# Larger transfers and merged DMA transposes in a one-core kernel for a speech joint network, forward and backward

The chip is one Trainium2, and the kernel uses one of its cores. The metric is device time in microseconds (us) of one execution on that core. Nearly all executions of one kernel fall within a few us; the few that are more than 1.5% above the fastest of their kernel are called slow and are left out of every comparison.

## The reference

The forward part is two convolutions over time with stride 2 and GELU, two projections, and a "joint" of every time step with every one of the 8 label positions `u`. The kernel returns this output and the gradients of all seven inputs, for a given `grad_out`.

```python
# x [2, 16000, 256], w1 and w2 [3, 256, 256], g [2, 8, 256], w_f, w_g, w_o [256, 256]; bf16
h  = gelu(conv(x, w1))[:, ::2]                  # 8000 steps
f  = gelu(conv(h, w2))[:, ::2]                  # 4000 steps
j  = tanh((f @ w_f)[:, :, None] + (g @ w_g)[:, None])
out = j @ w_o                                   # [2, 4000, 8, 256]
_, vjp = jax.vjp(forward, x, w1, w2, g, w_f, w_g, w_o)
return out, *vjp(grad_out)                      # grad_out [2, 4000, 8, 256]
```

## The kernel before

The 8000 rows of the joint are cut into 18 chunks (14 of 512 rows, two of 256, two of 160). A chunk has four pairs of `u`. For each pair, `grad_out` is loaded as rows (`GO_R`), which the gradient of `w_o` uses directly, and transposed by DMA into columns (`GOT`), which TensorE needs for the gradient of `j`. Rows of h, f and their gradients, needed for the weight gradients, are made by DMA transposes too. All these transposes are issued by one engine, SyncE (SP), one after the other.

The kernel orders its own instructions. Each operation is handed to a scheduler (`Flow`) with a cost in ns, and the scheduler simulates the engines and emits an order for each. The cost of a transpose is flat: 1260 ns, whatever its size.

```python
def dma(q, out, in_, r, w, bytes_, ..., transpose=False, ...):
    ...
    c = 1260.0 if transpose else 400.0 if q == "SP" else cost or (750.0 if q == "POOL" else 100.0)
    return op(q, c, go, r=r, w=w, ..., work=bytes_ / 256 * 1.25 if transpose else bytes_ / 300.0)
# ... cut: buffer classes, with their number of slots (some of 37)
("jt", 3), ("got", 3), ("go", 7), ("out", 6), ("rows", 4), ("hro", 2), ("hrs", 2), ("hre", 2), ("fr", 2),
# ... cut
def load_got(g_, up, h, at):            # half h (256 rows) of one pair of u: 8 blocks of 128x128
    if h == 0:
        S.setdefault("GOT", {})[up] = buf("got", [P, NB, 2, KT, P], BF16, "GOT")
    GOT, GO = S["GOT"][up], S["GO"][up, h]
    dma("SP", lambda: GOT[:, 2 * h:2 * h + 2].rearrange("p a u k q -> p (a u k) q"),
        lambda: GO[:].rearrange("p a u v -> p (a u v)"), r=[GO], w=[(GOT, h)], bytes_=2 * P * 1024,
        new=[GOT] if h == 0 else [], transpose=True, ...)

def load_gor(g_, up, h, at, hold=()):
    GO = buf("go", [P, 2, 2, V], BF16, "GO_R")
    # ... cut: one load of 256 KB per half
# ... cut: gradient of h, odd columns, in two products because the shifted block is a tile of its own
for q_, (lo, hi, in0) in enumerate(((0, P, lambda mt=mt: S["G1S"][:, mt, :]),
                                    (P, Ws, lambda mt=mt: S["G1o"][:, mt, r0:r0 + Ws - P]))):
    op("DVE", c_dve(hi - lo), ... scalar_tensor_tensor(out=GHo[:, mt, lo:hi], ...))
# ... cut: one transpose each for the rows of h (three) and of grad h (two)
GHoR = dma_rows("GHoR", "rows", g_, lambda: GHo[:]..., ghok, nb_of[g_])
GHeR = col_rows("GHeR", "rows", g_, GHe, ["z"])
```

## Time and profile before

| | before |
|---|---|
| median of 3 runs | 803.32 us (801.99 to 803.36) |
| span of the profiled execution | 800.2 us |
| TensorE busy, VectorE, ScalarE, GpSimd | 775.6, 754.2, 715.2, 223.2 us |
| SP queue taken by DMA issues, added up over the trace | 700.4 us, 494 issues |

This is SP's timeline before, around 120 us (columns: start, time that the issue took on the queue, operation, destination and source, count). "SPq" marks the queue itself.

```profile
113.86 3.74 SPq L438 DMA_TRANSPOSE GOT<-GO_R  x2
117.70 1.26 SPq L438 DMA_TRANSPOSE GHoR<-GHo  x1
119.02 1.34 SPq L438 DMA_TRANSPOSE GOT<-GO_R  x1
120.45 1.28 SPq L438 DMA_TRANSPOSE GHeR<-GHe  x1
121.83 3.79 SPq L438 DMA_TRANSPOSE GOT<-GO_R  x2
```

The halves of `GOT` stand between the other transposes, and the queue comes back to one of them every 5.2 us in the median over the run. The view of the tile `GOT` gives the issue times over the whole run (ns: least, median, most):

```profile
L438 SPq DMA_TRANSPOSE GOT<-GO_R x128: 1231/1436/4699, 19.4 to 765.8; - x128
```

### The profile page before, as it was taken

The numbers are of one execution on the slowest core, as the hardware profiler recorded it, in microseconds if no ns is written. First come the engines' busy times: TensorE is split into PE (matmuls) and PEld (weight loads), VectorE is DVE, ScalarE is ACT, GpSimd is POOL, SyncE is SP. The second block draws the span as 40 slices with busy tenths as digits, with TensorE's granted clock in tenths as the row PEclk, the third lists the DMA queues.
The fourth block names the chain that finished last, engine by engine and source line by source line (L and its number), as shares of the span: only waits on it lengthen the run. The fifth ranks groups of instructions, "written<-read, shape, count | busy, mean of one in ns | idle before, by whom it ended". The sixth has DMA issues, their size and how long they took to land.

```text
span 800.2 us, 17623 instructions
## 1 busy us (share of the span) xinstructions
PE 775.6 (97%) x6196; PEld 576.2 (72%) x6196; DVE 754.2 (94%) x1756; ACT 715.2 (89%) x1164; POOL 223.2 (28%) x461
## 2 busy tenths in 40 slices
PE   8788999999999999999999999999999999999997
PEld 6555667686776867787776668676776767778885
DVE  5999999998989999997989999999999999999995
ACT  5999999999898999997899999989898999898572
POOL 1212222321323122343232142222223122233242
PEclk9999999999999999999999999999999999999999
DMA  8999999999999998999999999999999999999984
GB/s 202 242 206 207 216 263 253 229 249 275 228 243 261 224 254 185 230 253 250 224 200 236 252 236 242 251 209 255 245 236 248 217 247 229 245 215 263 195 205 114
DMA packets 384700, 184.74 MB, mean 231 GB/s; under 512 B 331716, under 2 KB 368358, under 8 KB 384612
## 3 DMA queue, kind: packets, MB, share of 16 engines
q1 hardware_dynamic: 366644, 133.25, 85.8%
q0 software_dynamic: 15584, 49.19, 19.7%
q10 hardware_dynamic: 2384, 1.18, 0.6%
q8 instruction: 48, 0.79, 0.4%
q14 instruction: 40, 0.33, 0.1%
HBM read 52.48 MB, written 50.34 MB: 128 GB/s over the span
## 4 chain that ended last, share of the span: by engine, by line
PE 68%; DVE 19%; ACT 10%; issue 2%; DMA 1%; DVEq 0%; ACTq 0%
PE ps L412 58%; PE GWO L412 9%; DVE NGZ L833 4%; DVE ZS L841 3%; ACT JT L766 2%; DVE g_s L599 2%; DVE JR L779 2%; ACT JR L786 2%; DVE ACC L894 1%; ACT g_sq L595 1%; ACT JSQ L823 1%; DVE g_sq L610 1%; ACT g_s L605 1%; DVE GHo L954 1%; DMA XC<-in_x_dram 1%
## 5 line engine op out<-in xcount | busy, mean ns | idle before, releaser
L766 ACT ACTIVATE JT<-FE,GE 128x512 bf16<-128x512 bf16 (+2 forms) x288 | 182.0, 676 | 5.8 <-PE ps L412 5.6
L440 POOL DMA_DIRECT2D out_dram<-OUT_SB x136 | 95.2, 701 | 241.8 <-ACT OUT_SB L423 153.8
L412 PE MATMUL ps<-WO,JT 128*128 128x256 bf16 x1024 | 151.4, 272 | 2.7 <-DVE NGZ L833 0.8
L833 DVE SCALAR_TENSOR_TENSOR NGZ<-JSQ,ps 128x512 f32<-128x512 bf16 (+2 forms) x252 | 151.0, 605 | 2.0 <-PE ps L412 1.8
L412 PE MATMUL ps<-GOT,WT 128*128 128x512 bf16 (+3 forms) x640 | 151.0, 332 | 1.2 <-ACT HTe L597 0.5
L786 ACT ACTIVATE JR<-JR 128x1024 bf16<-128x1024 bf16 x128 | 136.4, 1070 | 6.6 <-DVE JR L779 6.5
L412 PE MATMUL GWO<-GO_R,JR 128*128 128x256 bf16 x1024 | 132.2, 273 | 3.3 <-ACT JR L786 3.3
L823 ACT ACTIVATE JSQ<-JT 128x1024 bf16<-128x1024 bf16 (+2 forms) x132 | 126.6, 960 | 7.7 <-DVE NGZ L833 5.7
L412 PEld LDWEIGHTS <-JT 128*128 128x128 bf16 x1024 | 98.4, 98 | 47.7 <-issue 5.7
L841 DVE TENSOR_TENSOR ZS<-ZS,NGZ 128x512 f32<-128x512 f32 (+2 forms) x216 | 131.1, 614 | 0.1
L423 ACT CAST OUT_SB<-ps 128x512 bf16<-128x512 f32 x208 | 119.2, 598 | 8.4 <-PE ps L412 8.2
L412 PEld LDWEIGHTS <-JR 128*128 128x128 bf16 x1028 | 99.5, 98 | 26.4 <-ACT JR L786 4.7
L412 PEld LDWEIGHTS <-WT 128*128 128x128 bf16 x1000 | 88.1, 98 | 37.3 <-issue 2.3
L412 PEld LDWEIGHTS <-W 128*128 128x128 bf16 x792 | 70.4, 99 | 56.8 <-issue 3.7
L412 PE MATMUL ps<-XC,W 128*128 128x512 bf16 (+4 forms) x432 | 94.2, 347 | 3.0 <-DMA XC<-in_x_dram 2.1
L779 DVE TENSOR_TENSOR JR<-FER,GEB 128x1024 bf16<-128x1024 bf16 x128 | 87.5, 685 | 0.1
L440 POOL DMA_DIRECT2D out_dram<-GX_SB x70 | 39.0, 558 | 159.6 <-ACT GX_SB L425 125.0
L412 PEld LDWEIGHTS <-X 128*128 128x128 bf16 x768 | 74.9, 98 | 10.8 <-DMA HRs<-HTo 0.2
L599 DVE SCALAR_TENSOR_TENSOR g_s<-g_sq,ps 128x512 bf16<-128x512 bf16 (+2 forms) x108 | 65.7, 609 | 11.7 <-ACT HTo L597 9.2
L412 PE MATMUL ps<-WT,GHo 128*128 128x256 bf16 x384 | 73.0, 273 | 0.2
L894 DVE TENSOR_TENSOR ACC<-ACC,ps 128x512 f32<-128x512 f32 x96 | 64.2, 677 | 9.2 <-PE ps L412 9.0
L595 ACT ACTIVATE g_sq<-ps 128x512 bf16<-128x512 f32 (+2 forms) x108 | 58.5, 546 | 10.1 <-PE ps L412 9.7
(137 smaller groups left out, 1281.5 us busy)
## 6 DMA issues: line engine op xcount, KB each, us to landing
GO_R<-in_grad_out_dram SPq DMA_DIRECT2D x120, 256.0 KB, 4.2
out_dram<-OUT_SB POOLq DMA_DIRECT2D x120, 256.0 KB, 4.8
X<-in_x_dram SPq DMA_DIRECT2D x28, 576.0 KB, 7.0
out_dram<-GX_SB POOLq DMA_DIRECT2D x60, 256.0 KB, 4.6
GOT<-GO_R SPq DMA_TRANSPOSE x128, 5.2
out_dram<-w_out SPq DMA_DIRECT2D x9, 128.0 KB, 2.1
GO_R<-in_grad_out_dram SPq DMA_DIRECT2D x8, 128.0 KB, 4.3
out_dram<-OUT_SB POOLq DMA_DIRECT2D x8, 128.0 KB, 3.8
```

Of the source, the lines that this page charges most:

```text
L412: nc.tensor.matmul(ps_ap, lhsT=lhsT, rhs=rhs, start=start, stop=stop)
L423: nc.scalar.copy(out=dst(), in_=src())
L440: return eng_.dma_start(out=out(), in_=in_())
L595: op("ACT", c_act(W, True), lambda e, mt=mt, ps=ps: nc.scalar.activation(out=sq[:, mt, :W], in_=ps[:, :W], func=ACT.Square, scale=GELU_SQR ...
L599: op("DVE", c_dve(W), lambda e, mt=mt, ps=ps: nc.vector.scalar_tensor_tensor(out=s[:, mt, :W], in0=sq[:, mt, :W], scalar=1.0, in1=ps[:, :W ...
L766: op("ACT", c_act(W, ptr=True), lambda e, j=j, mt=mt: nc.scalar.activation(out=JT[:, j, mt, :W], in_=S["FE"][:, mt, :W], func=ACT.Tanh, bi ...
L779: op("DVE", c_dve(n * 2 * D, 0.5), lambda e, lo=lo, n=n, m=m, JR=JR: nc.vector.tensor_tensor(out=JR[:m, lo % 2:lo % 2 + n], in0=S["FER"][: ...
L786: op("ACT", c_act(n * 2 * D), lambda e, lo=lo, n=n, m=m, JR=JR: nc.scalar.activation(out=JR[:m, lo % 2:lo % 2 + n], in_=JR[:m, lo % 2:lo % ...
L823: nc.scalar.activation(out=JSQ[:, :, :W], in_=JT[:, j, :, :W], func=ACT.Square)
L833: op("DVE", c_dve(W) + 6, lambda e, d2=d2, ps=ps, u=u, zap=zap, JSQ=JSQ: nc.vector.scalar_tensor_tensor(out=zap(), in0=JSQ[:, d2, :W], sca ...
L841: op("DVE", c_dve(W), lambda e, d2=d2, dst=dst, NGZ=NGZ: nc.vector.tensor_tensor(out=dst[:, d2, :W], in0=ZS[:, d2, :W], in1=NGZ[:, :W], op ...
L894: op("DVE", c_dve(512), lambda e: nc.vector.tensor_tensor(out=acc_ap().rearrange("p k d -> p (k d)"), in0=acc_ap().rearrange("p k d -> p ( ...
```

## The change

The intent is fewer and larger transfers. `grad_out`, its transpose and the output go by whole pairs of `u`, 512 rows at a time. Grad x is stored for two row blocks at once. The rows of h come out of one transpose of 18 blocks, and those of grad h out of one of 16. The block of h that is shifted by one column is kept in h's own tile, so convolution 2 reads it in one matmul and grad h is one product. Slots are recounted to fit the memory. The core of the diff:

```diff
-                    ("hto", 2), ("hs", 2), ... ("got", 3), ("go", 7), ("out", 6), ("rows", 4), ("hro", 2), ("hrs", 2), ("hre", 2), ("fr", 2) ...
+                    ("hh", 2), ... ("got", 3), ("go", 4), ("out", 3), ("rows", 2), ("ghr", 1), ("hr", 1), ("hrs", 1), ("fr", 1) ...
-    def load_got(g_, up, h, at):
-        dma("SP", lambda: GOT[:, 2 * h:2 * h + 2]..., lambda: GO[:]..., bytes_=2 * P * 1024, ...)
+    def load_got(g_, up, at):
+        S, n = st[g_], nb_of[g_]
+        GOT, GO = buf("got", [P, NB, 2, KT, P], BF16, "GOT"), S["GO"][up]
+        dma("SP", lambda: GOT[:, 0:n]..., lambda: GO[:, 0:n]..., bytes_=n * P * 1024, new=[GOT], transpose=True, ...)
-        GO = buf("go", [P, 2, 2, V], BF16, "GO_R")
+        GO = st[g_].setdefault("GO", {})[up] = buf("go", [P, NB, 2, V], BF16, "GO_R")
... (cut: out and grad x likewise)
+        HT = buf("hh", [P, KT * (2 * CW + P)], BF16, "HT")          # odd, shifted and even h in one tile
-        HRo = col_rows("HRo", "hro", g_, HTo, ["z"], late[0])
-        R0 = dma_rows("HRs", "hrs", g_, lambda: HS[:]..., [HS], 1, late[0])
-        HRe = col_rows("HRe", "hre", g_, HTe, ["z"], late[1])
+        dma("SP", lambda: HR.t[:, 0:ns + nc_]..., lambda: HT.t[:, 0:ns + nc_], r=[HT], w=[HR], ..., transpose=True, nb=late[0])
-        GHoR = dma_rows("GHoR", ...); GHeR = col_rows("GHeR", ...)
+        dma("SP", lambda: GHR.t[:, 0:2 * nc_]..., lambda: GH.t[:, 0:2 * nc_], r=ghk, w=[GHR], ..., transpose=True)
-            for q_, (lo, hi, in0) in enumerate(((0, P, ...G1S...), (P, Ws, ...G1o...))):
-                op("DVE", c_dve(hi - lo), ...)
+            op("DVE", c_dve(Ws), ...)
```

## The prediction

> **What bounds the kernel now.** I read the page first (busy shares, slices, chain of waits), then the busy time by stretches of 20 us, then the waits of TensorE and of the SP queue, then single tiles.
>
> The page's busy shares, its two slice rows for TensorE and DMA, and its chain:
>
> ```profile
> span 800.2 us, 17623 instructions
> PE 775.6 (97%) x6196; PEld 576.2 (72%) x6196; DVE 754.2 (94%) x1756; ACT 715.2 (89%) x1164; POOL 223.2 (28%) x461
> ...
> PE   8788999999999999999999999999999999999997
> ...
> DMA  8999999999999998999999999999999999999984
> ...
> PE 68%; DVE 19%; ACT 10%; issue 2%; DMA 1%; DVEq 0%; ACTq 0%
> ```
>
> TensorE is busy 775.6 of 800.2 us. DMA is as full as TensorE in these rows, but holds 1% of the chain: transfers arrive in time. The by-stretch view (columns: stretch and length, then TensorE, weight loads, VectorE, ScalarE, GpSimd, granted clock, DMA share, GB/s) shows where TensorE's missing 24.6 us are:
>
> ```profile
> 0.00:20.00 20.00, 16.37 (x141) 12.47 (x142) 10.02 (x33) 11.11 (x24) 3.52 (x16) 0.91 0.83 202
> 20.00:40.00 20.00, 15.86 (x123) 10.88 (x121) 19.49 (x55) 20.00 (x39) 5.16 (x10) 1.00 1.16 242
> 40.00:60.00 20.00, 17.23 (x130) 11.71 (x129) 19.64 (x55) 19.61 (x33) 3.24 (x8) 1.00 0.96 206
> 60.00:80.00 20.00, 17.46 (x131) 11.94 (x130) 20.00 (x46) 19.70 (x30) 4.67 (x10) 1.00 1.04 207
> ...
> 780.00:800.00 20.00, 14.77 (x139) 11.41 (x136) 11.50 (x31) 4.71 (x10) 5.74 (x14) 0.98 0.44 115
> ```
>
> The first four stretches lack 3.6 + 4.1 + 2.8 + 2.5 = 13.0 us, the last 5.2; the 700 us between lack 6.4. From 20 to 80 us VectorE and ScalarE are full, and TensorE waits for them. TensorE's waits name only two on a DMA:
>
> ```profile
> PE GWO L412 <- ACT JR L786: 3.3, 3, 1.5
> PE psb L652 <- DVE FE L428: 3.2, 4, 1.6
> ...
> PE ps L412 <- DMA XC<-in_x_dram: 2.1, 1, 2.1
> ...
> PE ps L412 <- DMA GOT<-GO_R: 0.4, 1, 0.4
> ```
>
> The 2.1 us are the very first load of x, which the change leaves alone. So what this change makes cheaper, transfers, costs TensorE 0.4 us that can be seen.
>
> [...] six 512-column matmuls starting at 499.64 are followed by the next group at 500.93, so 1.29 / 6 = 215 ns[...]. [...] start and end (about 7 us before the first x is in, some 5 at the end) can't be streamed over.
> [...] grad_out loads land after 4.2 us at 256 KB and still 3.8 us at 32 KB.
> [...]
> [...] the grad-h product takes 277 ns at 128 columns, 543 at 384 and 677 at 512, so a line of 1.04 ns per column over about 144 ns.
>
> **The change, part by part** (18 chunks: 14 of 512 rows, two of 256, two of 160).
> - *Fewer grad_out loads and transposes.* 136 loads become 80 (14 x 4 + 2 x 4 + 2 x 4 x 2) and 128 transposes 72. A load issue takes 0.53 us and a transpose at least 1.23 us of the SP queue even for few blocks (the 16-block one of x 1.46), so SP gets back about 56 x 0.53 + 56 x 1.2 = 97 us. The merged h transposes take 58 issues to 22, grad h 36 to 18: 54 x 1.2 = 65 us. SP spends much of its time waiting for others (79.0 us for the matmuls ahead of transposes alone), and TensorE loses 0.4 us to it. Worth: about 0.
> - *Fewer stores.* Out stores go from 136 (701 ns of GpSimd) to 80, large grad x stores from 60 (558 ns) to about 30. From 256 against 128 row pieces I get 143 ns per 128 pieces, so a doubled out store is about 1.0 us; GpSimd saves roughly 95 - 56 x 1.0 - 24 x 0.6 = 25 us plus 15 us. It is busy 28% and mostly waits for ScalarE's output. Worth: about 0.
> - *The shifted block in h's own tile.* Convolution 2 streams one 512-column matmul where it had 128 + 384: 72 fewer matmuls, same columns[...].
> - *grad h (odd) in one product.* Per full chunk and half 277 + 543 becomes 677 ns: 143 ns; 36 of them are 5.2 us of VectorE's 754. VectorE holds 19% of the chain; 0.19 x 5.2 = 1.0 us, and in the last chunk, where this product stands alone on the chain, 272 + 178 becomes about 310: 0.1 us. Worth: about 1.1 us.
> - *The end.* The two last grad-h transposes are issued at 787.64 and 788.93 and the last gradients wait for both; one issue saves up to 1.2 us, of which its longer flight takes some back. Worth: 0.5 us.
> - *Buffers.* 7 half slots of grad_out become 4 whole ones, 6 of out become 3, so a chunk of 256 or 160 rows, which fills only half a slot or less, now has 4 in place of 7. Before, SP issues seven grad_out loads at 13 to 18 us: four for chunk 0 and three for chunk 1. Now chunk 0 takes all four, and chunk 1's first must wait for the first gradient-of-w_o matmuls (25 to 26 us). Behind that SP is in two x transposes until 33.7, then come a load (about 5 us) and a transpose (about 6): ready at about 45 us, first used at 50.6 now. It just fits, or costs 1 to 4 us in the stretch where VectorE and ScalarE are already the limit. I book 1.5 us.
> Sum: -0.2 - 1.1 - 0.5 + 1.5 = about -0.3 us on the span. The instruction order is also made anew by the kernel's own scheduler, whose model of transfers changes; that moves things by a few us either way, without a sign I can give. The reported 803.32 is itself one of 801.99 to 803.36, with the profiled run at 801.93. Prediction: 801.0 us, a trifle better as the buffer cost may not show.
>
> **Rivals.**
> - *DMA relief is worth more than it looks.* For: DMA is at nine tenths in nearly all slices, and transposes at times hold SP for 2.8 us (median of those of x), a sign of a full path. Against: bytes are the same, the packets under 512 B (331716 of 384700) come from the transposes and are not made larger, and TensorE waits 0.4 us. Were all of TensorE's 6.4 us gaps in the middle due to it, the time would be 795.
> - *Buffers become the bound.* Coarser slots (out, grad_out, one slot each for the h, grad-h and f rows) make TensorE wait at each chunk. For: fewer slots, held for a whole pair. Against: a pair lasts 12 us (48 us per chunk over 4), an out slot is held 12 + 5 us, and three slots give 36; the h rows are loaded about a chunk ahead and read in the first third of the next. If it bit in all 18 chunks by 1 us: 819.
> - *VectorE was the true limit.* Then the whole 5.2 us come off: 796. Against: in the middle TensorE shows 20.00 of 20 in most stretches.
>
> **Range and chances.** Faster by over 2% means under 787: two thirds of all of TensorE's idle time gone, from a change that touches 0.4 us of its waits: 0.03. Slower by over 2% means 16 us of new waits, only by the buffer rival in most chunks: 0.07. The rest, 0.90. The range of 791 to 811 leaves 10 us each way for the new order and the start.
>
> **What would show each step right or wrong.** Right: TensorE busy at 774 to 777 us; 72 fewer matmuls; VectorE down by 5 us to about 749; GpSimd down by 30 to 45; SP issues nearly halved with no wait of TensorE on them. The start is right if the stretches 20 to 60 lack 6 to 11 us. Wrong if the waits show TensorE on grad_out's transposes or on DMA for more than 3 us (buffers), or if the stretches between 120 and 780 lack clearly more or less than 5 us. A gap that repeats once per chunk would refute me most.

## The result, and the profile after

The changed kernel takes 812.14 us (median of 4 runs, 808.41 to 814.33), against 803.34 us (801.99 to 804.06) for the kernel before, run on the same chip. The ratio is 1.0107, with a 95% interval of 1.0067 to 1.0147. All ratios here are the mean time of one kernel's fast runs over that of the other's of the same rounds, so they are not quite the ratios of the medians quoted. It counts as "same" at 2%, but it is 1% slower and lies 1.1 us above the predicted range. The profiled execution, at 814.33 us, is the slowest of the four, and that of the kernel before, at 801.93 us, among its fastest: the spans compared below differ by 12.4 us, the medians by 8.8.

The page after:

```profile
span 812.6 us, 16872 instructions
PE 780.9 (96%) x6124; PEld 575.1 (71%) x6124; DVE 744.4 (92%) x1710; ACT 716.5 (88%) x1179; POOL 154.2 (19%) x370
...
PE 42%; DVE 25%; ACT 22%; DMA 5%; issue 5%; SPq 1%; DVEq 0%; ACTq 0%
```

There are 72 fewer matmuls, as planned, and 10 and 69 us less work on VectorE and GpSimd. Yet TensorE is busy for 5.3 us longer, and its share of the chain fell from 68 to 42%. The stretches of 20 us (stretch and length, then TensorE, weight loads, VectorE, ScalarE, GpSimd, granted clock, DMA share, GB/s) show one place, first after and then before:

```profile
120.00:140.00 20.00, 15.76 (x133) 12.73 (x131) 16.62 (x37) 18.25 (x27) 2.88 (x6) 1.00 1.17 182
140.00:160.00 20.00, 18.96 (x105) 10.67 (x106) 14.83 (x30) 14.05 (x23) 2.27 (x5) 0.83 1.06 262
```

```profile
120.00:140.00 20.00, 20.00 (x166) 15.81 (x165) 19.20 (x40) 19.30 (x31) 5.11 (x8) 1.00 1.12 253
140.00:160.00 20.00, 20.00 (x136) 12.70 (x135) 19.29 (x44) 19.07 (x30) 6.06 (x13) 1.00 1.05 229
```

Before, TensorE worked through all 40 us at full clock. After, it lacks 4.24 and 1.04 us, and in the second stretch the mean clock is 0.83. TensorE's waits and its timeline name what it lacked (in brackets: idle time just before, and what ended it):

```profile
PE ps L412 <- DMA GOT<-GO_R: 5.3, 1, 5.3
```

```profile
141.04 1.03 PE L412 MATMUL ps<-GOT,WT 128*128 128x512 bf16 x2 [5.28 <-DMA GOT<-GO_R]
```

It is a single wait of 5.28 us for a transposed pair of `grad_out`. The records of the granted clock show 6.8 us at half speed from 140.0 on, 4.2 us into the wait. In the 5.8 us of it that lie after the wait, matmuls of 512 columns start 427 ns apart, against 216 ns in the microseconds after; these 5.8 us cost another 2.9 us, as an estimate (half of them). SP's timeline shows why the pair was late:

```profile
116.06 3.59 SPq L438 DMA_TRANSPOSE GHR<-GH  x1
119.75 1.25 SPq L438 DMA_TRANSPOSE FR<-FT  x1
121.05 0.58 SPq L440 DMA_DIRECT2D GO_R<-in_grad_out_dram  x1
121.73 4.53 SPq L438 DMA_TRANSPOSE HR<-HT  x1
126.36 9.43 SPq L438 DMA_TRANSPOSE GOT<-GO_R  x1
```

Everything that the issue at 126.36 had to wait for had happened by 119.70 (read from the semaphores in the trace). So it stood behind the merged transposes of grad h and h, and then took 9.43 us itself. What made it take so long can be read in part from GpSimd's timeline, which shows three stores of 512 KB in the 7 us around:

```profile
122.11 0.59 POOL L440 DMA_DIRECT2D out_dram<-GX_SB  x1 [6.40 <-ACT GX_SB L425]
123.07 0.71 POOL L440 DMA_DIRECT2D out_dram<-OUT_SB  x1 [0.37 <-ACT OUT_SB L423]
128.13 0.55 POOL L440 DMA_DIRECT2D out_dram<-GX_SB  x1 [4.36 <-DVE ZS L863]
```

The packets of the DMA engines, which the trace also keeps (128 packets of 256 bytes are one block of a transpose), show these stores moving from 125 to 140 us without a break. From 126 to 138 us the transposes advanced by 1.5 blocks per us, against 3.0 over the whole run. Such slow spells are general here. Between 60 and 760 us, in the microseconds in which any transpose ran, 4.5 blocks per us moved before and 5.2 after where no store did, and 1.9 before but 1.3 after where stores held over half of the engines' time. So the change's larger stores are part of the setting of the stall.

The tile's issue times after:

```profile
L438 SPq DMA_TRANSPOSE GOT<-GO_R x72: 1237/3758/9427, 17.4 to 781.2; - x72
```

Twice the size (16 of the 72 still have 8 blocks) has 2.6 times the median. Added up over the trace, SP's issues took 688.2 us for 328 transfers, against 700.4 us for 494 before. So 166 fewer issues gave back 12 us: the 56 fewer loads of `grad_out` 39 us, while the transposes, 110 fewer, took 24 us more (586.4 to 610.4), and the loads of x 3 us more. Per block of 128x128 the transposes took 0.24 to 0.25 us of the queue in both kernels, each with about 2460 blocks.

Where did the 12.4 us of span go? TensorE's idle time rose by 7.1 us: -0.9 in the first 80 us, +6.4 from 80 to 780 us (5.3 of it the one wait), +1.7 at the end. Its busy time rose by 5.3 us. The clock was at half for 13.8 us of the span, against 4.5 us before, and half of that difference, 4.6 us, is the most that it can have added.

### The profile page after: what moved, and what is told of

The parts are those of the page before. It is cut to its first block, busy times and chain, and to the rows that moved or that the text cites.

```text
span 812.6 us, 16872 instructions
## 1 busy us (share of the span) xinstructions
PE 780.9 (96%) x6124; PEld 575.1 (71%) x6124; DVE 744.4 (92%) x1710; ACT 716.5 (88%) x1179; POOL 154.2 (19%) x370
## 4 chain that ended last, share of the span: by engine, by line
PE 42%; DVE 25%; ACT 22%; DMA 5%; issue 5%; SPq 1%; DVEq 0%; ACTq 0%
PE ps L412 35%; PE GWO L412 6%; DVE NGZ L855 4%; ACT JT L788 4%; ACT JR L808 4%; DVE g_s L603 4%; DVE ZS L863 3%; ACT OUT_SB L423 3%; ACT JSQ L845 2%; ACT g_sq L599 2%; DMA GOT<-GO_R 2%; ACT GX_SB L425 2%; DVE g_sq L614 2%; DVE JR L801 1%; ACT g_s L609 1%
## 5 line engine op out<-in xcount | busy, mean ns | idle before, releaser
L788 ACT ACTIVATE JT<-FE,GE 128x512 bf16<-128x512 bf16 (+2 forms) x288 | 189.9, 705 | 1.5 <-DVE FE L428 1.5
L808 ACT ACTIVATE JR<-JR 128x1024 bf16<-128x1024 bf16 x128 | 139.5, 1100 | 9.8 <-DVE JR L801 9.6
L845 ACT ACTIVATE JSQ<-JT 128x1024 bf16<-128x1024 bf16 (+2 forms) x120 | 118.9, 991 | 16.2 <-DVE NGZ L855 15.4
L423 ACT CAST OUT_SB<-ps 128x512 bf16<-128x512 f32 x204 | 123.8, 614 | 8.6 <-PE ps L412 8.5
L412 PEld LDWEIGHTS <-W 128*128 128x128 bf16 x720 | 66.2, 98 | 55.0 <-issue 3.3
L440 POOL DMA_DIRECT2D out_dram<-OUT_SB x80 | 54.3, 679 | 259.6 <-ACT OUT_SB L423 173.7
L412 PE MATMUL ps<-WT,GH 128*128 128x256 bf16 x732 | 97.9, 275 | 0.2
L412 PE MATMUL ps<-GHR,X 128*128 128x256 bf16 x768 | 92.0, 273 | 0.4 <-DVE NGZ L855 0.4
L412 PEld LDWEIGHTS <-GH 128*128 128x128 bf16 x732 | 72.0, 99 | 12.4 <-DVE GH L971 0.4
L603 DVE SCALAR_TENSOR_TENSOR g_s<-g_sq,ps 128x512 bf16<-128x512 bf16 (+2 forms) x108 | 66.2, 613 | 15.3 <-ACT HT L601 12.7
L599 ACT ACTIVATE g_sq<-ps 128x512 bf16<-128x512 f32 (+2 forms) x108 | 62.2, 576 | 15.8 <-PE ps L412 15.3
```

What stands on the lines that cost most here:

```text
L412: nc.tensor.matmul(ps_ap, lhsT=lhsT, rhs=rhs, start=start, stop=stop)
L423: nc.scalar.copy(out=dst(), in_=src())
L440: return eng_.dma_start(out=out(), in_=in_())
L599: op("ACT", c_act(W, True), lambda e, mt=mt, ps=ps: nc.scalar.activation(out=sq[:, mt, :W], in_=ps[:, :W], func=ACT.Square, scale=GELU_SQR ...
L603: op("DVE", c_dve(W), lambda e, mt=mt, ps=ps: nc.vector.scalar_tensor_tensor(out=s[:, mt, :W], in0=sq[:, mt, :W], scalar=1.0, in1=ps[:, :W ...
L788: op("ACT", c_act(W, ptr=True), lambda e, j=j, mt=mt: nc.scalar.activation(out=JT[:, j, mt, :W], in_=S["FE"][:, mt, :W], func=ACT.Tanh, bi ...
```

## The experiments

Three theories stood after the result.
- **M**, the order: the scheduler charges a flat 1260 ns per transpose, so it doesn't see that a merged one takes twice as long, and queues too much ahead of an urgent one.
- **S**, the size: a 16-block transpose holds the queue and lands late as one piece.
- **B**, the buffers: four whole slots of `grad_out` for seven halves leave too little room.

A fourth, **T**, came later: any order is a draw from a lottery, and the kernel before had been tuned to a good one.

### First three runs

`a_cost158`: the changed kernel, charged by block, so that the order is made anew.

```diff
-        c = 1260.0 if transpose else ...
+        c = max(1260.0, bytes_ / 32768 * 157.5) if transpose else ...
```

> The changed kernel with one number of its own scheduler altered: a transpose is charged to the SP queue by its blocks (157.5 ns each, so 1260 ns for 8 blocks and 2520 for 16) and no longer a flat 1260 ns whatever its size. Transfers, buffers and arithmetic are as in the changed kernel; only the order of instructions can differ. Theory M (the flat charge made the scheduler believe that the merged transposes cost the SP queue half, so that it lines them up too late): the 5.3 us wait of TensorE for GOT at 141 us and the half clock after it are gone, time 800 to 805. Theory S (the 16-block transfer itself is the trouble: its first half can't be used before its second has landed) and theory B (coarser buffers): a wait of 3 us or more for GOT stays, 808 to 814.

Measured: 806.15 us (804.58 to 810.12), ratio 1.0064 [1.0030, 1.0099]. The long wait is gone in its profile, which M wanted, but the time is above M's range and below that of S and B.

`a_halves`: the changed kernel in exactly its own order on every engine; each 16-block transpose of `grad_out` is issued as two of 8, back to back.

```diff
+                eng_.dma_start_transpose(out=o_[:, 0:n // 2], in_=i_[:, 0:n // 2 * P])
+                return eng_.dma_start_transpose(out=o_[:, n // 2:n], in_=i_[:, n // 2 * P:n * P])
```

> The changed kernel in its own order, but each 16-block transpose of grad_out is issued as two of 8 blocks, one right after the other, into the two halves of the same tile. Theory S: the first half lands some 4 us earlier, but the matmuls read the whole tile, so at best the second half lands a little earlier by pipelining: the wait for GOT falls to 3 us or less, time 805 to 809. Theory M: the queue is behind by its order and its bytes, and these are the same: the wait stays within 4 to 7 us, time 808 to 815. Issue time: if the cost went per issue, two of 8 blocks would occupy SP for more than one of 16 (2 x 1.85 against 3.9 us by the two profiles: no difference).

Measured: 807.66 us (806.02 to 810.08), ratio 1.0078 [1.0046, 1.0110]. The longest wait on `GOT` was 1.83 us. That pleased S, but a later run took most of it back.

`b_cheap`: the kernel before, with the charge made too low for its own 8-block transposes.

```diff
+        c = 1260.0 * min(1.0, bytes_ / 524288) if transpose else ...
```

> The kernel before, with its scheduler's charge for a transpose made too small in the same proportion: 78.75 ns per block, so 630 ns for 8 blocks and, as before, 1260 for 16. Transfers and buffers are those of the kernel before. Theory M: the order turns as optimistic as that of the changed kernel, a wait of TensorE on a transpose of 2 us or more appears, 806 to 815. Theories S and B: nothing changes but the luck of the order, 800 to 806 and less than 1 us of waits on GOT.

Measured: 807.17 us (805.15 to 807.59), ratio 1.0064 [1.0035, 1.0094], with a wait of 3.15 us on `GOT` at 28 us. An order made with too low a charge can slow the kernel before as well.

### A control, both cures, and a neutral step

`c_after`: the changed kernel unchanged, as a control.

> The changed kernel itself again, on whatever chip this call gets, as the control for the other runs of this call. Both theories: 808 to 814 us, ratio 1.008 to 1.014 to the kernel before, and TensorE's wait of 4 to 7 us on the transposed grad_out near 141 us is there again, because the order of the instructions on each queue is fixed when the kernel is built. If the wait is gone, it was an accident of one execution and the explanation by queue order falls.

Measured: 810.98 us (806.31 to 816.27), ratio 1.0101 [1.0059, 1.0144]. The loss is there again, but not at the same place. I had expected the wait near 141 us; it was near 744 us:

```profile
744.51 0.61 PE L412 MATMUL ps<-GOT,WT 128*128 128x256 bf16 x2 [9.91 <-DMA GOT<-GO_R]
```

```profile
711.01 9.28 SPq L438 DMA_TRANSPOSE GHR<-GH  x1
720.34 0.58 SPq L440 DMA_DIRECT2D GO_R<-in_grad_out_dram  x1
721.03 1.27 SPq L438 DMA_TRANSPOSE FR<-FT  x1
722.39 8.67 SPq L438 DMA_TRANSPOSE HR<-HT  x1
731.15 4.66 SPq L438 DMA_TRANSPOSE GOT<-GO_R  x1
```

This is the same sequence, a chunk's merged transposes and then an urgent `GOT`, with the length now in the merged ones. The clock was at half for 10.2 us from 737.0 on, 2.4 us into the wait of 9.91 us. The order of the program is fixed and such a sequence comes in every full chunk, so two executions can stall in different chunks, where the transposes happen to take long. The six fast executions fall into two groups, 806.3 to 807.7 and 814.3 to 816.3 us. The 8 us between them is about what the first stall cost with its half clock (5.3 + 2.9). The profiled execution is from the upper group.

`c_halves158` (both cures of the first runs) and `c_pieces158` (the same order, with the transposes of h and grad h in pieces of at most 8 blocks as well):

> The changed kernel with both cures together: its own scheduler charges the transpose queue 157.5 ns per 128x128 block instead of a flat 1260 ns per transfer, and every 16-block transpose of grad_out is issued as two of 8 blocks back to back. Theory M+S (the loss is the flat charge and the long 16-block transposes): 802 to 805 us, ratio 1.000 to 1.005, no wait of more than 1.5 us on transposed grad_out. Rival B (the buffers, counted by whole pairs, and the reordering that comes with them cost the rest): 806 to 809 us, no better than either cure alone (806.15 and 807.66), ratio 1.006 to 1.009.

Measured: 805.80 us (803.62 to 807.98), ratio 1.0035 [1.0014, 1.0056].

> As the run before it, and the merged transposes of h (18 blocks) and of grad h (16 blocks) are issued in pieces of at most 8 blocks too; buffers and order as in that run. If long transposes are what hurts: 801 to 804 us, 1 to 2 us better than with grad_out's alone. If only the transposes that TensorE waits for soon matter (grad_out's), the same within 1 us. If pieces cost the queue something each (34 more issues at 1.2 us or so, hidden so far), still no more than 1 us.

Measured: 803.69 us (803.08 to 810.22), ratio 1.0023 [0.9994, 1.0053]. Neither profile has a wait of 1.5 us on `GOT`. Together the cures win most of the loss back.

`b_1500`: the kernel before, with a flat 1500 in place of 1260.

> The kernel before with only the scheduler's flat charge moved from 1260 to 1500 ns per transpose: no buffer, transfer or instruction changes, only the order in which the scheduler places them. It measures what a reordering without any reason costs. Theory T (the kernel before sits on a tuned order, and any other order costs some 0.5%): 804 to 807 us, ratio 1.004 to 1.008. Theory M (only a charge that is too low hurts, and 1500 is nearer to the measured mean of 1.85 us): 799 to 803 us, ratio 0.997 to 1.002.

Measured: 801.31 us (800.32 to 802.80), ratio 0.9979 [0.9957, 1.0000]. This new order doesn't cost the kernel before anything, which speaks against T. (Over all runs, two of its four new orders are level, this one and `b_late240`, and two cost 0.6 and 0.7%, `b_cheap` and `b_cost240`. So an order can cost half of the loss by itself.)

### Pieces alone, and a fuller charge

`e_pieces`: the changed kernel in exactly its own order, all merged transposes in pieces of at most 8 blocks.

```diff
+                cut = [n * k // -(-n // 8) for k in range(-(-n // 8) + 1)]
+                for lo, hi in zip(cut, cut[1:]):
+                    x_ = eng_.dma_start_transpose(out=o_[:, lo:hi], in_=i_[:, lo * P:hi * P])
```

> The changed kernel with its own order on every engine and the flat charge kept; only, every merged transpose (transposed grad_out, h, grad h) is issued in pieces of at most 8 blocks, back to back. So buffers, buffer counts and order are those of the change. Theory S (long transposes hold the queue, 9.28 and 8.67 us for one of 16 and one of 18 blocks just before the stall of the control run): 804 to 808 us, ratio 1.003 to 1.008, no wait of TensorE on transposed grad_out of more than 3 us. Theory M (only the order made with the flat charge matters): 808 to 812 us, ratio 1.008 to 1.012. Rival B (buffers by whole pairs) says as M.

Measured: 813.50 us (808.65 to 822.30, one slow run), ratio 1.0116 [1.0081, 1.0151]. S alone falls: in the same order, shorter pieces win nothing. Pieces sent back to back hold the queue as long as large transfers do (626 us for all transposes of this profile, 610 for those of the changed kernel). What its slow executions wait for I can't show, since the profiled one was lucky (span 806.9 us, 2.4 us of waits on `GOT`).

`e_pieces240` and `b_cost240`: 240 ns per block, about the measured rate, in the pieces version and in the kernel before.

> As the best version so far (pieces of at most 8 blocks, charge by block), with 240 ns charged per block instead of 157.5, which is what a block took on the queue in the profiles (about 590 us for some 2460 blocks). Theory M (a truer charge gives a better order): 800 to 803 us, ratio 0.997 to 1.001. If the charge was good enough at 157.5, and the rest is reordering without reason: 802 to 806 us.

Measured: 812.97 us (812.12 to 820.43), ratio 1.0138 [1.0104, 1.0171].

> The kernel before with only the scheduler's charge changed, to 240 ns per block and at least 1260 ns (8 blocks: 1920, 16 blocks: 3840). If the truer charge helps the kernel before as it helped the changed one: 797 to 800 us, ratio 0.993 to 0.998, better than the flat 1500 (0.9979). If its 8-block transfers were placed well enough already: 800 to 804 us, ratio 0.998 to 1.003.

Measured: 809.38 us (807.28 to 810.09), ratio 1.0073 [1.0048, 1.0097]. Both were misses: the truer charge made things worse. The profile of `e_pieces240`, the slowest of its executions, has a wait of 5.1 us for weights at its start and one of 4.6 us on `GOT` at 297 us: pieces of at most 8 blocks don't rule the stall out. The waits of `b_cost240` show the start too:

```profile
PE psb L1135 <- DMA W<-in_w_dram: 4.5, 1, 4.5
```

The new order begins with a long wait for weights. To see how far TensorE was behind, I subtracted the nominal time of the matmuls already started from the time since the start (nominal was my estimate for each form; the medians of start to start in the trace before, 109 ns at 256 columns and 216 at 512 among them, give the same 13.7 us below for that kernel; 39 matmul records that are missing from the trace of `b_cost240` are counted in). By 80 us `b_cost240` was 7.8 us further behind than before. From there to 790 us it lost 11.4 us, against 13.7 us before. So in `b_cost240` the charge did its harm at the start.

### The charge by block only after the first chunk

```diff
+        c = (1260.0 if (F.now if at is None else at) < 300.0 else max(1260.0, bytes_ / 32768 * 240.0)) if transpose else ...
```

`b_late240` is the kernel before with this line:

> The kernel before with 240 ns charged per block for work dated after the first chunk. The run with 240 throughout lost 8 us in its first 80 us (a wait of 4.5 us on weights among them) and then was 2.3 us better than before up to 790 us, counted as time without matmul work. If that loss belongs to the start alone: 797 to 800 us, ratio 0.994 to 0.998. If the order of the start and of the rest cannot be separated: 801 to 806 us.

Measured: 801.97 us (800.47 to 803.77), ratio 1.0001 [0.9990, 1.0012]. The loss of `b_cost240` was the start, as said, but the gain I hoped for didn't come.

`a_late240` is the changed kernel with it, its transfers whole:

> The changed kernel with its own transfers (16- and 18-block transposes whole, buffers by pairs); only the scheduler charges the transpose queue 240 ns per block, and only for work dated after the first chunk, so the start is ordered as in the change. If the change itself is neutral, as predicted, and the loss is the order made with a flat 1260 ns: 800 to 804 us, ratio 0.997 to 1.003. If the long transposes or the coarser buffers cost by themselves: 805 to 810 us, ratio 1.004 to 1.010.

Measured: 804.65 us (801.24 to 812.63), ratio 1.0053 [1.0023, 1.0084]. Again there are two groups: seven executions from 801.2 to 804.7 us and four from 809.9 to 812.6 us. The profiled one is from the lower group and waits 0.8 us on `GOT`. So this order makes the stall rarer and doesn't end it. My first expectation, that the change would be neutral in a good order, was a miss.

`a_1500` and `a_2000` are the changed kernel with other flat charges:

> The changed kernel with a flat 1500 ns per transpose instead of 1260: what the same small step did to the kernel before (0.9979). If the place of the loss is chance of the order (theory T: any order is a draw, some 0.5% apart): anything from 802 to 812 us. If the flat charge must be near the measured mean (3.9 us for 16 blocks) to help: 808 to 812 us, ratio 1.008 to 1.012, as the control.

Measured: 808.84 us (804.38 to 818.53, one slow run), ratio 1.0075 [1.0046, 1.0105]. Its profile has a wait of 6.5 us on `GOT` at 651 us with 6.8 us at half clock.

> The same with a flat 2000 ns. Theory M (the order gets better as the charge nears what a merged transpose takes): between the control (1.010) and the charge by block (1.0064), 804 to 808 us, and better than with 1500. Theory T: anything from 802 to 812 us, without order by charge.

Measured: 812.50 us (811.99 to 814.59), ratio 1.0131 [1.0114, 1.0147]. There is no trend with the flat charge, so M in its simple form, the higher the better, falls too. Five orders of the changed kernel with whole transposes have now been run, and all cost 0.5 to 1.3%.

### Which part: undo it, and do it alone

`u_go`: the changed kernel with the loads and transposes of `grad_out` in halves again, in seven half slots, flat charge; everything else as changed.

```diff
-    def load_got(g_, up, at):
-    def load_gor(g_, up, at, hold=()):
+    def load_got(g_, up, h, at):             # both as in the kernel before
+    def load_gor(g_, up, h, at, hold=()):
-    ("go", 4)
+    ("go", 7)
-    mm(GWO[:, d2, :], ..., GO[:m, tb, j, :], ...)
+    mm(GWO[:, d2, :], ..., GO[:m, tb % 2, j, :], ...)
```

> The changed kernel with one part undone: grad_out is loaded and transposed in halves again, with seven half buffers, flat charge as in the change; merged h and grad-h transposes, pair stores and two-block grad x stay. If grad_out's pairing (long transposes just where TensorE waits for them, and four whole buffers) is the culprit: 801 to 804 us, ratio 0.999 to 1.003, and no run 8 us above the others. If the merged transposes of h and grad h that stand before it on the queue do it alone: 806 to 811 us, ratio 1.006 to 1.011.

Measured: 801.12 us (798.71 to 811.06, one slow run of 22), ratio 0.9991 [0.9973, 1.0008]. The whole loss is gone. Its executions spread widely (the fast ones up to 807.72), and the sign "no run 8 us above the others" failed once, with the slow run. SP's timeline has the interleaving again, though the merged transposes of h and grad h are still whole:

```profile
710.13 3.11 SPq L438 DMA_TRANSPOSE GHR<-GH  x1
713.34 1.21 SPq L440 DMA_DIRECT2D GO_R<-in_grad_out_dram  x2
714.60 1.88 SPq L438 DMA_TRANSPOSE GOT<-GO_R  x1
716.59 2.19 SPq L438 DMA_TRANSPOSE FR<-FT  x1
718.88 0.55 SPq L440 DMA_DIRECT2D GO_R<-in_grad_out_dram  x1
719.52 1.28 SPq L438 DMA_TRANSPOSE GOT<-GO_R  x1
720.85 4.75 SPq L438 DMA_TRANSPOSE HR<-HT  x1
725.70 2.37 SPq L438 DMA_TRANSPOSE GOT<-GO_R  x1
```

`b_go`: the kernel before with that part alone (five out slots in place of six, for the room).

> The kernel before with that part alone: grad_out by pairs with four whole buffers (five out buffers instead of six, for the room). If grad_out's pairing is the culprit: 807 to 813 us, ratio 1.006 to 1.012, with executions in two groups some 8 us apart. If it needs the merged transposes of h and grad h before it on the queue: 800 to 804 us.

Measured: 805.32 us (803.51 to 808.05), ratio 1.0033 [1.0023, 1.0043], in one group. Pairing `grad_out` costs a third of a per cent here, with one out slot fewer and a new order, and a whole one beside the rest of the change. Both expectations were partly missed: it needs the others for its full cost, and it isn't free without them.

`p_late240`: the order of `a_late240` exactly, with pieces of at most 8 blocks.

> The changed kernel with pieces of at most 8 blocks and 240 ns charged per block after the first chunk: the late-charge run (1.0053, 4 of its 11 executions 8 us above the rest) with the long transposes taken away. If a long transpose is what makes those executions slow once the order is good: 801 to 804 us, ratio 0.999 to 1.003, no second group. If pieces change nothing, as with the flat charge: 803 to 807 us with a second group near 811.

Measured: 803.35 us (802.53 to 806.32), ratio 1.0002 [0.9983, 1.0021], in one group. In this order the pieces are worth 0.5% and the upper group is gone. It keeps the change's four whole slots, so B isn't needed. Its profile, the slowest of its 14 executions, still has waits of 1.9 and 1.5 us on `GOT`.

`u_go_late240`: `u_go` with the late charge.

> The first run's kernel with the charge of 240 ns per block after the first chunk. If both grad_out's pairing and the flat charge matter: 799 to 802 us, ratio 0.996 to 1.000, the candidate to be level with the kernel before or better. If the merged transposes cost by themselves whatever the order: 804 to 808 us.

Measured: 803.09 us (802.31 to 805.52), ratio 1.0004 [0.9985, 1.0023]. In its profile SP's issues take only 648.5 us, 52 less than before, and of those transposed pairs whose landing is recorded after 60 us (30 of 72; 17 before), all land at least 6.5 us ahead of their first use (2.3 us before). It is no faster for that.

The grid of ratios for the changed kernel, each against the kernel before on the same chip. Within a row the order on every engine is the same, except in the last column:

| order made with | whole | grad_out in 2 pieces | all in pieces of 8 or less | grad_out in halves from the load on |
|---|---|---|---|---|
| flat 1260 (the change) | 1.0107, 1.0101 | 1.0078 | 1.0116 | 0.9991 |
| 157.5 per block | 1.0064 | 1.0035 | 1.0023 | |
| 240 per block, after chunk 0 | 1.0053 | | 1.0002 | 1.0004 |

No version beat the kernel before by more than its interval; the best two are `b_1500` at 0.9979 and `u_go` at 0.9991.

## Why the prediction was wrong

Its main reading was right: TensorE's own stream sets the time, and cheaper transfers gained nothing. In the trace before, consecutive matmuls start 109 ns apart at 256 columns, 216 at 512, 163 at 384 and 56 at 128 (medians). With all 6196 at the median of their form that is an estimate of 762 us, 95% of the span of 800.2 us. What cheaper transfers are worth, `u_go_late240` shows best, with 52 us off the queue and no gain.

The step that failed is the worth given to "Fewer grad_out loads and transposes": "Worth: about 0". Undoing this part alone (`u_go`, with its buffers and in a new order) moves the ratio from 1.0107 and 1.0101 to 0.9991. So in this kernel the pairing cost about 1%, 8 to 9 us, and the profile shows the way: a wait of 5.3 us and an estimated 2.9 us of half clock behind it, at a place where the prediction had counted on TensorE losing 0.4 us.

Under it lies an error in the sum. "SP gets back about 56 x 0.53 + 56 x 1.2 = 97 us", with 65 us more for the h and grad-h transposes, took the least time of a `GOT` issue, 1.23 us, for a cost per issue. The loads did give back 39 us (30 booked), but the transposes took 24 us more, where 132 less were booked: 12 us in all, not 162. The trace before held the warning, 1231 to 4699 ns for issues of one size. By the packets of both traces, counted between 20 and 330 us, a median of 12 blocks was outstanding when an issue of more than 2 us ended (the middle halves: 9.5 to 12.1 and 10.4 to 12.7). My reading is that a long issue lasts until about so many blocks are left, its own or earlier ones, so its time goes with blocks and with how fast they drain. That booking did not move the predicted time by itself, since it was given no worth, but it hid what a merged transpose does to the one behind it: a pair of `grad_out` lands 7.1 us after its issue in the median (5.2 before), behind merged transposes that took up to 9.3 us each (in the control), and there is no half of it to slip between them. The loss isn't the work but its grain.

The other steps:
- **Matmuls**: 72 fewer, right. The 0.2 us for them in the sum was my estimate; the medians of the trace before (56 and 163 ns in two matmuls, 216 in one) give 72 x 3 ns, an estimate of 0.2 us too. TensorE's busy time was wrong (780.9, not 774 to 777); the half clock can have added up to 4.6 us of it.
- **grad h in one product**: right in size per instruction (277 + 543 became 679 ns). VectorE fell by 9.8 us rather than 5.2; among other moves, the new order gave 24 evacuations of grad x from it to ScalarE (113 there after, 89 before). It was worth nothing visible.
- **GpSimd**: mis-sized. It fell by 69 us, not 40; a doubled out store took 0.72 us in the mean where I had estimated 1.0 us, no more than a single one (also 0.72).
- **Buffers at the start**: the 1.5 us I booked did not come. The stretches from 20 to 60 us lack 6.8 us, against 6.9 before.
- **The end**: not the gain of 0.5 us; TensorE lacks 1.7 us more there.
- **Signs of error**: the first was met, a wait of more than 3 us on transposed `grad_out`. The prediction put "(buffers)" beside it, and no run bears that out: `p_late240` has these buffers and is level. The second was met too: the stretches between 120 and 780 us lack 11.8 us, not about 5.
- **The centre**: the sum of -0.3 us on the median of 803.32 gives 803.0; 801.0 leans on the single profiled execution (801.93).
- **The new order**: "moves things by a few us either way, without a sign I can give". For these coarser pieces it has a sign: six runs with whole transposes in five orders were all slower.

Four things stay open. That the upper group of executions consists of those with a stall is supported by the profiles of the control, of `a_1500` and of `a_late240`, but timed executions have no profile, so it is not shown. What slowed the executions of `e_pieces` is not seen. How the rest of the loss, beside pairing alone (0.3%), is shared by merged h and grad h and by the larger stores was not tested: no run undoes the stores alone. They can't do it alone, since `u_go` keeps them and is level, but transposes moved more slowly beside them (1.3 blocks per us, against 1.9 before). And since each version ran in one order or two, part of any difference between versions can be the draw of the order (T).

## What to carry to other kernels

Merging transfers on a queue that one engine needs promptly makes the unit of waiting larger, and this can cost more than the saved issues (here 166 fewer issues gave back 12 us of the queue, and pairing `grad_out` cost 8 to 9 us of time); look at whether an issue's time is fixed or goes with size before counting issues as savings. If the program schedules itself, change its cost model together with the sizes, and keep the piece that the bound engine waits for small enough to slip between the others. Judge such a change on many executions: one profile of the changed kernel showed a stall at 141 us and the next one at 744 us, and its executions differ by up to 10 us.
